# Gate and up in pairs of column slices over four k tiles, and attention's small matmuls packed into parts of the array

## The chip, the cores and the metric

The kernel runs on one core of one Trainium2 chip. The metric is the device time of one execution in microseconds (us). TensorE is PE in the profile, VectorE is DVE, ScalarE is ACT, GpSimd is POOL; PEld is the loading of weights into TensorE, which mostly runs beside the matmul before. PSUM is the memory into which this kernel's matmuls write; a place there for 512 float32 columns is called a bank here.

## The reference, cut to what matters

Four layers over x of shape 1 x 2048 x 576: attention A, MLP B, A, B, each on a layernorm of x and added to x. A is a sliding-window attention with 32 heads of 18, eight keys per query at distances 0, 2, ..., 14. B multiplies two projections, without a nonlinearity:

```python
def _B_ref(x, w_gate, w_up, w_down):          # D = 576, F = 4608
    g = jnp.einsum("bsd,df->bsf", x, w_gate)  # contraction over all 576
    u = jnp.einsum("bsd,df->bsf", x, w_up)
    h = g * u
    return jnp.einsum("bsf,fd->bsd", h, w_down)
x = x + _A_ref(_layernorm(x), A_wqkv, A_wo)
x = x + _B_ref(_layernorm(x), B_w_gate, B_w_up, B_w_down)
# ... and both once more
```

The inputs: w_gate and w_up are normal numbers times 0.05 times 576^-0.5, w_down times 0.05 times 4608^-0.5, so B adds very little to x.

## The kernel before

Tokens are worked on in chunks of 256 (CH), of two tiles of 128 (NST). 576 input features are five k tiles of 128 (KT = 5), of which the fifth holds 64 features (TL) and 64 columns that are zero in xn. F is 36 slices of 128 (NFT), called ft. The attention of one chunk is issued ahead of the MLP of another, so that their instructions are interleaved on every engine: TensorE fills with MLP matmuls while VectorE does the attention's elementwise work.

```python
# head: layernorm, transpose to xnT (features on partitions)
nc.scalar.activation(xn[:, 0:D], x[:], ACT.Identity, bias=nmr[:], scale=rstd[:])
for k in range(KT):
    nc.tensor.transpose(tps[:, k, :], xn[:, k * P:(k + 1) * P], ident[:])
nc.scalar.copy(xnT[:, :, i * P:(i + 1) * P], tps[:])
# ... attention: qkv, then per pair of window taps: products and sums on DVE, logits on PE
    nc.tensor.matmul(pa[b][:], lhsT=Erep2, rhs=s1[...], start=True, stop=True)
    for j in range(4):
        nc.scalar.copy(Lt[32 * j:32 * j + 32, ...], lgv[32 * j:32 * j + 32, :, SQ * j:SQ * (j + 1)])
# ... softmax, then the weights are broadcast over the heads' features
for j in range(4):
    b = next_pa()
    nc.tensor.matmul(pa[b][:], lhsT=Bsel[:, j]..., rhs=a_c[...], start=True, stop=True)
    nc.scalar.copy(ab[:, :, j, :], pa[b][:]...)
# ... weighted sum of v over the taps on DVE (pv, oT), then wo
# MLP
def gate_up(ft):
    ps = gu[ft % 2]                            # two PSUM banks, gate and up in one
    for (hh, w_) in ((0, wg), (1, wu)):
        for k in range(KT):
            nc.tensor.matmul(ps[:, hh, :], lhsT=w_[:, k, ft * P:(ft + 1) * P], rhs=xnT[:, k, :], ...)
    nc.scalar.copy(g_sb[:], ps[:, 0, :])
    nc.vector.tensor_tensor(hT[:], ps[:, 1, :], g_sb[:], op=ALU.mult)
def down(ft):
    for i in range(NST):                       # 512 + 64 output columns
        nc.tensor.matmul(accm[i][:], lhsT=hT[:, i * P:(i + 1) * P], rhs=wdt[:, ft % G, 0:512], ...)
        nc.tensor.matmul(acct[:, i, :], lhsT=hT[:, i * P:(i + 1) * P], rhs=wdt[:, ft % G, 512:D], ...)
gate_up(0)
for ft in range(1, NFT):
    gate_up(ft)
    down(ft - 1)
```

## Time and profile before

| | kernel before |
|---|---|
| time, median of 4 executions | 1268.28 us |
| span of the profiled execution | 1265.2 us |
| PE, DVE, ACT busy | 93%, 59%, 44% |
| gate and up matmuls | 5760 of 256 columns |
| waiting PE after the start-up | 81 of 1188 us |

The last row is not a line of any view. It comes from the trace: for each matmul the time from its start to the next matmul's start, less its step (0.109 us for 256 columns and so on, as the prediction derives it). I call the surplus a gap and name it after the matmul that follows. Streaming is the sum of the steps alone; packed matmuls that start together count as one step. Some traces lack matmul records (159 of 10032 in this one); their steps are put back. The count is finer than the profile's idle column, because the record of a matmul, 273 ns for 256 columns, covers 0.16 us beyond its step and hides short gaps.

### The profile page before, as it was taken

The page shows a single profiled execution, that of the slowest core. Times are in us where ns is not written, and L with a number is a line of the kernel's source. Part 1 is how long each engine was busy: PE and PEld are TensorE (multiplying, and loading weights), DVE is VectorE, ACT ScalarE, POOL GpSimd, SP SyncE. Part 2 cuts the span into 40 slices and gives each one's busy share as a digit, 9 for nine tenths or more (in the row PEclk, how much of TensorE's full clock was granted, in tenths as well). Part 3 has the DMA queues.
Part 4 walks back from the last instruction along what each step waited for, and adds up shares of the span by engine and source line. Part 5 has one row for each costly group of instructions (what it writes and reads, how often), then busy time and mean ns, then how long its engine had stood idle before and what let it go on. Part 6 is the DMA issues. An engine that isn't in the chain of part 4 may idle for free.

```text
span 1265.2 us, 24030 instructions
## 1 busy us (share of the span) xinstructions
PE 1176.8 (93%) x9873; PEld 874.7 (69%) x10032; DVE 745.3 (59%) x1602; ACT 559.7 (44%) x1523; POOL 4.8 (0%) x23
## 2 busy tenths in 40 slices
PE   3289999999999999999999999999999999999998
PEld 2056767767676776767677677776767777676776
DVE  4657375674737558375675736658484655837532
ACT  6263353545345354454634435354544534445321
POOL 1000000000000000000000000000000000000000
PEclk9589999999999999999999999999999999999999
DMA  7912213122231212312222231222223132221331
GB/s 265 296 28 76 81 56 92 57 76 76 76 109 57 80 57 76 95 57 76 76 76 68 75 94 57 76 67 68 83 76 81 62 88 64 76 80 57 91 103 48
DMA packets 83918, 105.95 MB, mean 84 GB/s; under 512 B 3424, under 2 KB 81888, under 8 KB 82528
## 3 DMA queue, kind: packets, MB, share of 16 engines
q1 hardware_dynamic: 83808, 104.41, 27.9%
q8 instruction: 78, 1.28, 0.4%
q14 instruction: 32, 0.26, 0.1%
HBM read 102.04 MB, written 2.36 MB: 83 GB/s over the span
## 4 chain that ended last, share of the span: by engine, by line
PE 53%; DVE 34%; ACT 10%; issue 2%; DMA 0%; SPq 0%; ACTq 0%; DVEq 0%
PE gu L299 28%; PE accm L312 10%; PE pa L201 8%; DVE oT L266 7%; DVE pv L265 7%; DVE prod L216 5%; DVE hT L305 5%; ACT ab L255 3%; PE pa L272 3%; PE acct L314 3%; PE tps L184 2%; ACT Lt L225 2%; DVE prod L217 2%; DVE st L172 1%; ACT xnb L182 1%
## 5 line engine op out<-in xcount | busy, mean ns | idle before, releaser
L305 DVE TENSOR_TENSOR hT<-gu,g_sb 128x256 bf16<-128x256 f32 x576 | 241.5, 419 | 310.8 <-ACT g_sb L304 309.9
L299 PE MATMUL gu<-xnT,wg 128*128 128x256 bf16 x2880 | 423.3, 273 | 0.0
L299 PE MATMUL gu<-xnT,wu 128*128 128x256 bf16 x2880 | 419.1, 273 | 0.0
L304 ACT CAST g_sb<-gu 128x256 bf16<-128x256 f32 x576 | 213.2, 370 | 429.2 <-PE gu L299 420.0
L312 PE MATMUL accm<-wdt,hT 128*128 128x512 bf16 x1001 | 325.0, 381 | 9.2 <-DVE hT L305 7.1
L299 PEld LDWEIGHTS <-wg 128*128 128x128 bf16 x2880 | 245.0, 98 | 90.3 <-issue 0.2
L299 PEld LDWEIGHTS <-wu 128*128 128x128 bf16 x2880 | 280.6, 98 | 36.9 <-issue 1.2
L314 PE MATMUL acct<-wdt,hT 128*128 128x64 bf16 x1152 | 221.9, 193 | 11.2 <-DVE hT L305 3.6
L312 PEld LDWEIGHTS <-hT 128*128 128x128 bf16 x1152 | 112.2, 97 | 119.2 <-DVE hT L305 40.6
L216 DVE TENSOR_TENSOR prod<-qT,kT 128x2560 bf16<-128x2560 bf16 x64 | 93.2, 1484 | 102.0 <-ACT kT L206 102.0
L201 PE MATMUL pa<-xnT,wqkv 128*128 128x256 bf16 x1200 | 144.5, 273 | 1.9 <-ACT xnT L185 1.5
L201 PEld LDWEIGHTS <-wqkv 128*128 128x128 bf16 x1200 | 117.0, 98 | 29.1 <-issue 4.5
L314 PEld LDWEIGHTS <-hT 128*128 128x128 bf16 x1152 | 112.8, 98 | 9.9 <-issue 2.0
L266 DVE TENSOR_TENSOR oT<-oT,pv 128x1280 bf16<-128x1280 bf16 x112 | 91.2, 814 | 0.7
L265 DVE TENSOR_TENSOR pv<-vT,ab 128x1280 bf16<-128x1280 bf16 x112 | 89.6, 815 | 0.0
L225 ACT COPY Lt<-pa 32x128 f32<-32x128 f32 x256 | 65.6, 256 | 34.8 <-PE pa L222 31.6
L182 ACT ACTIVATE xnb<-xf,nmr,rstd 128x576 bf16<-128x576 f32 x64 | 55.5, 869 | 11.5 <-DVE nmr L179 11.1
L272 PE MATMUL pa<-wo_p,oT 128*128 128x288 bf16 x320 | 46.1, 292 | 14.0 <-DVE oT L266 12.3
L185 ACT COPY xnT<-tps 128x640 bf16<-128x640 bf16 x64 | 44.1, 689 | 21.5 <-PE tps L184 20.4
L172 DVE BATCH_NORM_STATS2 st<-xf 128x6 f32<-128x288 f32 x128 | 51.6, 439 | 2.9 <-ACT xf L74 2.9
L184 PE MATMUL tps<-ident,xnb 128*128 128x128 bf16 x320 | 29.8, 226 | 22.2 <-ACT xnb L182 19.1
L272 PEld LDWEIGHTS <-oT 128*128 128x128 bf16 x320 | 30.5, 99 | 28.6 <-DVE oT L266 19.1
(57 smaller groups left out, 538.0 us busy)
## 6 DMA issues: line engine op xcount, KB each, us to landing
wdt<-in_B_w_down_dram SPq DMA_DIRECT2D x144, 576.0 KB, 4.0
wg<-in_B_w_gate_dram SPq DMA_DIRECT2D x4, 1152.0 KB, 9.4
wu<-in_B_w_up_dram SPq DMA_DIRECT2D x4, 1152.0 KB, 22.7
xb<-in_A_x_dram SPq DMA_DIRECT2D x16, 144.0 KB, 3.6
out_dram<-ob SPq DMA_DIRECT2D x16, 144.0 KB, 3.9
wraw<-in_A_wqkv_dram SPq DMA_DIRECT2D x4, 432.0 KB, 5.0
wg<-in_B_w_gate_dram SPq DMA_DIRECT2D x2, 576.0 KB, 17.0
wu<-in_B_w_up_dram SPq DMA_DIRECT2D x2, 576.0 KB, 23.9
```

The source lines that it names most:

```text
L182: nc.scalar.activation(xn[:, 0:D], x[:], ACT.Identity, bias=nmr[:], scale=rstd[:])
L201: nc.tensor.matmul(pa[b][:, 0:CH], lhsT=wqf[:, k, t3, t * P:(t + 1) * P], rhs=xnT[:, k, :], start=(k == 0), stop=(k == KT - 1))
L216: nc.vector.tensor_tensor(prod[:], q2, k2, op=ALU.mult)
L225: nc.scalar.copy(Lt[32 * j:32 * j + 32, 2 * p_:2 * p_ + 2, :], lgv[32 * j:32 * j + 32, :, SQ * j:SQ * (j + 1)])
L265: nc.vector.tensor_tensor(pv[:], vT[:, :, o0:o0 + CH], abw, op=ALU.mult)
L266: nc.vector.tensor_tensor(oT[:], oT[:], pv[:], op=ALU.add)
L272: nc.tensor.matmul(pa[hh][:, 0:HD], lhsT=oT[:, t, i * P:(i + 1) * P], rhs=wo_p[:, t, hh * HD:(hh + 1) * HD], start=(t == 0), stop=(t == KT ...
L299: nc.tensor.matmul(ps[:, hh, :], lhsT=w_[:, k, ft * P:(ft + 1) * P], rhs=xnT[:, k, :], start=(k == 0), stop=(k == KT - 1), skip_group_chec ...
L304: nc.scalar.copy(g_sb[:], ps[:, 0, :])
L305: nc.vector.tensor_tensor(hT[:], ps[:, 1, :], g_sb[:], op=ALU.mult)
L312: nc.tensor.matmul(accm[i][:], lhsT=hT[:, i * P:(i + 1) * P], rhs=wdt[:, ft % G, 0:512], start=(ft == 0), stop=(ft == NFT - 1))
L314: nc.tensor.matmul(acct[:, i, :], lhsT=hT[:, i * P:(i + 1) * P], rhs=wdt[:, ft % G, 512:D], start=(ft == 0 and i == 0), stop=(ft == NFT - ...
```

## The change

Its visible intent: make gate and up cheaper, with one copy and one product for two ft; use narrow matmuls in parts of the array for the logits and the broadcast of the softmax weights; lay the 64-feature tails of gate and up out in two halves of one tile. Cut to its core:

```diff
-    wu = wpool.tile([P, KT, F], BF16, name="wu")
+    wu = wpool.tile([P, KT - 1, F], BF16, name="wu")
+        nc.sync.dma_start(wg[0:TL, KT - 1, :], B_w_gate[(KT - 1) * P:D, :])
+        nc.sync.dma_start(wg[TL:P, KT - 1, :], B_w_up[(KT - 1) * P:D, :])
-    gu = [psum.tile([P, 2, CH], FP32, name=f"gu{i}") for i in range(2)]
+    gp = psum.tile([P, 2, CH], FP32, name="gp")
+    up = psum.tile([P, 2, CH], FP32, name="up")
             nc.scalar.activation(xn[:, 0:D], x[:], ACT.Identity, ...)
+            nc.gpsimd.tensor_copy(xn[:, D:DP], xn[:, D - TL:D])
 # logits: one group of four after all taps
-            nc.tensor.matmul(pa[b][:], lhsT=Erep2, rhs=s1[...], ...)
-            for j in range(4):
-                nc.scalar.copy(Lt[32 * j:32 * j + 32, ...], ...)
+        for j in range(4):
+            nc.tensor.matmul(pa[b][32 * j:32 * j + 32, :], lhsT=Esum, rhs=s1[:, :, SQ * j:SQ * (j + 1)], ...)
+        nc.scalar.copy(Lt[:], pa[b][:]...)
 # broadcast: 32 contraction rows each
-        for j in range(4): ... lhsT=Bsel[:, j] (128 rows) ...
+        for j2 in range(0, 4, 2):
+            for j in (j2, j2 + 1):
+                nc.tensor.matmul(pa[j % 2][:], lhsT=Brep[32 * j:32 * j + 32]..., rhs=a_c[32 * j:32 * j + 32]..., ...)
 # MLP
+        def gate_up(f2):
+            for ps, w_ in ((gp, wg), (up, wu)):
+                for e in range(2):
+                    for k in range(KT - 1):
+                        nc.tensor.matmul(ps[:, e, :], lhsT=w_[:, k, fs], rhs=xnT[:, k, :], ...)
+                nc.scalar.copy(g_sb[:], gp[:])
+                nc.vector.tensor_tensor(hT[:], up[:], g_sb[:], op=ALU.mult)
```

More of the change, by code (lines that the diff above doesn't have):

```diff
@@ L85 @@
     xn_bufs = [st_pool.tile([P, DP], BF16, name=f"xnb{i}") for i in range(2)]
-    for t_ in xn_bufs:
-        nc.gpsimd.memset(t_[:, D:DP], 0.0)
     wqkv = wpool.tile([P, KT, 3, DHP, 32], BF16, name="wqkv")
@@ L91, with load_rows @@
     wg = wpool.tile([P, KT, F], BF16, name="wg")
-    wu = wpool.tile([P, KT, F], BF16, name="wu")
+    wu = wpool.tile([P, KT - 1, F], BF16, name="wu")
     ksz = [min(P, D - k * P) for k in range(KT)]
     TL = D - (KT - 1) * P
-    def load_rows(dst, src):
-        for k in range(KT):
-            nc.sync.dma_start(dst[:ksz[k], k, :], src[k * P:k * P + ksz[k], :])
-        nc.sync.dma_start(dst[TL:2 * TL, KT - 1, :], src[(KT - 1) * P:D, :])
+    def load_rows(dst, src, lo=0):
+        for k in range(KT - 1):
+            nc.sync.dma_start(dst[:, k, :], src[k * P:(k + 1) * P, :])
+        nc.sync.dma_start(dst[lo:lo + TL, KT - 1, :], src[(KT - 1) * P:D, :])
     startup_pool = tc.tile_pool(name="startup", bufs=1)
@@ L112 @@
     if nlayers > 1:
-        load_rows(wg, B_w_gate)
-        load_rows(wu, B_w_up)
+        for k in range(KT - 1):
+            nc.sync.dma_start(wg[:, k, :], B_w_gate[k * P:(k + 1) * P, :])
+        nc.sync.dma_start(wg[0:TL, KT - 1, :], B_w_gate[(KT - 1) * P:D, :])
+        nc.sync.dma_start(wg[TL:P, KT - 1, :], B_w_up[(KT - 1) * P:D, :])
+        for k in range(KT - 1):
+            nc.sync.dma_start(wu[:, k, :], B_w_up[k * P:(k + 1) * P, :])
     wd_v = B_w_down.rearrange("(g t p) d -> g p t d", p=P, t=G)
@@ L133 @@
     Erep = consts.tile([P, 4, 32], BF16, name="Erep")
-    Erep2 = Erep[:].rearrange("p a b -> p (a b)")
-    Bsel = consts.tile([P, 4, 4, 32], BF16, name="Bsel")
+    Esum = Erep[:, 0, :]
+    Brep = consts.tile([P, 4, 32], BF16, name="Brep")
     n_alayers = (nlayers + 1) // 2
@@ L143, in finish_startup @@
         nc.gpsimd.memset(wqkv[:, :, :, Dh:DHP, :], 0.0)
+        nc.gpsimd.memset(wqkv[TL:P, KT - 1, :, 0:Dh, :], 0.0)
         for t_ in halo_k + halo_v:
@@ L146, in finish_startup @@
         for k in range(KT):
-            src = wraw[:, k, :].rearrange("p (t h d) -> p t d h", t=3, h=H)
+            kk = ksz[k]
+            src = wraw[:kk, k, :].rearrange("p (t h d) -> p t d h", t=3, h=H)
             if k % 2 == 0:
-                nc.vector.tensor_copy(wqkv[:, k, :, 0:Dh, :], src)
+                nc.vector.tensor_copy(wqkv[:kk, k, :, 0:Dh, :], src)
             else:
-                nc.scalar.copy(wqkv[:, k, :, 0:Dh, :], src)
+                nc.scalar.copy(wqkv[:kk, k, :, 0:Dh, :], src)
         startup_pool.__exit__(None, None, None)
@@ L156, in finish_startup @@
                                     base=-32 * g0, pattern=[[0, 4], [-1, 32]], channel_multiplier=1)
-        nc.gpsimd.memset(Bsel[:], 0.0)
-        for j in range(4):
-            nc.gpsimd.affine_select(out=Bsel[:, j], in_=Bsel[:, j], compare_op=ALU.not_equal, fill=1.0,
-                                    base=-32 * j, pattern=[[0, 4], [-1, 32]], channel_multiplier=1)
+        nc.gpsimd.tensor_copy(Brep[:], Erep[:])
         rot_box["rot"] = ctx.enter_context(tc.tile_pool(name="rot", bufs=2))
@@ L209, in phase_A @@
         nc.scalar.copy(halo_v[la][:], vT[:, :, CH:CH + HALO])
+        s1 = rot_box["rot"].tile([P, W, CH], BF16, name="s1", bufs=1)
         for p_ in range(W // 2):
@@ L217, in phase_A @@
             nc.vector.tensor_tensor(prod[:, :, 0:4:2, :], prod[:, :, 0:4:2, :], prod[:, :, 1:4:2, :], op=ALU.add)
-            s1 = rot_box["rot"].tile([P, 2, CH], BF16, name="s1", bufs=2)
-            nc.vector.tensor_tensor(s1[:], prod[:, :, 0, :], prod[:, :, 2, :], op=ALU.add)
-            nc.vector.tensor_tensor(s1[:], s1[:], prod[:, :, 4, :], op=ALU.add)
-            b = next_pa()
-            nc.tensor.matmul(pa[b][:], lhsT=Erep2, rhs=s1[:].rearrange("p w s -> p (w s)"), start=True, stop=True)
-            lgv = pa[b][:].rearrange("p (w s) -> p w s", w=2)
-            for j in range(4):
-                nc.scalar.copy(Lt[32 * j:32 * j + 32, 2 * p_:2 * p_ + 2, :], lgv[32 * j:32 * j + 32, :, SQ * j:SQ * (j + 1)])
-            yield
-            yield
+            s1v = s1[:, 2 * p_:2 * p_ + 2, :]
+            nc.vector.tensor_tensor(s1v, prod[:, :, 0, :], prod[:, :, 2, :], op=ALU.add)
+            nc.vector.tensor_tensor(s1v, s1v, prod[:, :, 4, :], op=ALU.add)
+            yield
+        b = next_pa()
+        for j in range(4):
+            nc.tensor.matmul(pa[b][32 * j:32 * j + 32, :], lhsT=Esum, rhs=s1[:, :, SQ * j:SQ * (j + 1)],
+                             start=True, stop=True)
+        nc.scalar.copy(Lt[:], pa[b][:].rearrange("p (w s) -> p w s", w=W))
+        yield
         if c == 0:
@@ L250, in phase_A @@
         yield
-        for j in range(4):
-            b = next_pa()
-            nc.tensor.matmul(pa[b][:], lhsT=Bsel[:, j].rearrange("p a b -> p (a b)"),
-                             rhs=a_c[:].rearrange("p w s -> p (w s)"), start=True, stop=True)
-            nc.scalar.copy(ab[:, :, j, :], pa[b][:].rearrange("p (w s) -> p w s", w=W))
+        for j2 in range(0, 4, 2):
+            for j in (j2, j2 + 1):
+                nc.tensor.matmul(pa[j % 2][:], lhsT=Brep[32 * j:32 * j + 32].rearrange("p a b -> p (a b)"),
+                                 rhs=a_c[32 * j:32 * j + 32].rearrange("p w s -> p (w s)"), start=True, stop=True)
+            for j in (j2, j2 + 1):
+                nc.scalar.copy(ab[:, :, j, :], pa[j % 2][:].rearrange("p (w s) -> p w s", w=W))
         yield
@@ L289, in phase_B @@
         wds = {}
-        def gate_up(ft):
-            if ft % G == 0:
-                wdt = rot_box["rot"].tile([P, G, D], BF16, name="wdt", bufs=3)
-                nc.sync.dma_start(wdt[:], wd_v[ft // G])
-                wds[ft // G] = wdt
-            ps = gu[ft % 2]
-            for (hh, w_) in ((0, wg), (1, wu)):
-                for k in range(KT):
-                    nc.tensor.matmul(ps[:, hh, :], lhsT=w_[:, k, ft * P:(ft + 1) * P], rhs=xnT[:, k, :],
-                                     start=(k == 0), stop=(k == KT - 1), skip_group_check=True)
-            g_sb = rot_box["rot"].tile([P, CH], BF16, name="g_sb", bufs=2)
-            hT = rot_box["rot"].tile([P, CH], BF16, name="hT", bufs=3)
-            with tc.high_priority():
-                nc.scalar.copy(g_sb[:], ps[:, 0, :])
-                nc.vector.tensor_tensor(hT[:], ps[:, 1, :], g_sb[:], op=ALU.mult)
-            hts[ft] = hT
@@ L308, in down @@
-        def down(ft):
-            hT = hts.pop(ft)
-            wdt = wds[ft // G]
-            for i in range(NST):
-                nc.tensor.matmul(accm[i][:], lhsT=hT[:, i * P:(i + 1) * P], rhs=wdt[:, ft % G, 0:512],
-                                 start=(ft == 0), stop=(ft == NFT - 1))
-                nc.tensor.matmul(acct[:, i, :], lhsT=hT[:, i * P:(i + 1) * P], rhs=wdt[:, ft % G, 512:D],
-                                 start=(ft == 0 and i == 0), stop=(ft == NFT - 1), skip_group_check=True)
+        def gate_up(f2):
+            for ft in (2 * f2, 2 * f2 + 1):
+                if ft % G == 0:
+                    wdt = rot_box["rot"].tile([P, G, D], BF16, name="wdt", bufs=3)
+                    nc.sync.dma_start(wdt[:], wd_v[ft // G])
+                    wds[ft // G] = wdt
+            for ps, w_ in ((gp, wg), (up, wu)):
+                for e in range(2):
+                    fs = slice((2 * f2 + e) * P, (2 * f2 + e + 1) * P)
+                    for k in range(KT - 1):
+                        nc.tensor.matmul(ps[:, e, :], lhsT=w_[:, k, fs], rhs=xnT[:, k, :],
+                                         start=(e == 0 and k == 0), stop=(k == KT - 2), skip_group_check=True)
+            g_sb = rot_box["rot"].tile([P, 2, CH], BF16, name="g_sb", bufs=2)
+            hT = rot_box["rot"].tile([P, 2, CH], BF16, name="hT", bufs=3)
+            with tc.high_priority():
+                nc.scalar.copy(g_sb[:], gp[:])
+                nc.vector.tensor_tensor(hT[:], up[:], g_sb[:], op=ALU.mult)
+            hts[f2] = hT
@@ new lines, in down @@
+        def down(f2):
+            hT = hts.pop(f2)
+            for e in range(2):
+                ft = 2 * f2 + e
+                wdt = wds[ft // G]
+                for i in range(NST):
+                    nc.tensor.matmul(accm[i][:], lhsT=hT[:, e, i * P:(i + 1) * P], rhs=wdt[:, ft % G, 0:512],
+                                     start=(ft == 0), stop=(ft == NFT - 1))
+                    nc.tensor.matmul(acct[:, i, :], lhsT=hT[:, e, i * P:(i + 1) * P], rhs=wdt[:, ft % G, 512:D],
+                                     start=(ft == 0 and i == 0), stop=(ft == NFT - 1), skip_group_check=True)
@@ L317, in phase_B @@
         gate_up(0)
         yield
-        for ft in range(1, NFT):
-            gate_up(ft)
-            down(ft - 1)
+        for f2 in range(1, NFT // 2):
+            gate_up(f2)
+            down(f2 - 1)
             yield
-        down(NFT - 1)
+        down(NFT // 2 - 1)
         for i in range(NST):
@@ L385 @@
                 n += 1
-                if n == (NFT * 2) // 3 and k + 1 < nB:
+                if n == NFT // 3 and k + 1 < nB:
                     b_head(k + 1)
```

## The prediction

> **What bounds the kernel now.** I read the page first (busy shares, slices, groups), then the timeline of TensorE in a calm stretch, then the waits, then the windows of one layer period. The busy shares and slices of the page:
>
> ```profile
> PE 1176.8 (93%) x9873; PEld 874.7 (69%) x10032; DVE 745.3 (59%) x1602; ACT 559.7 (44%) x1523; POOL 4.8 (0%) x23
> ...
> PE   3289999999999999999999999999999999999998
> ...
> PEclk9589999999999999999999999999999999999999
> ```
>
> TensorE (PE) is full from slice 3 on, at full clock; only the first 73 us (the first attention body has nothing beside it) are thin. A busy PE can still be a waiting PE, so I look at the steps between matmuls. The timeline of PE in a calm stretch:
>
> ```profile
> 212.22 0.38 PE L312 MATMUL accm<-wdt,hT 128*128 128x512 bf16 x1
> 212.44 0.19 PE L314 MATMUL acct<-wdt,hT 128*128 128x64 bf16 x1
> 212.47 0.38 PE L312 MATMUL accm<-wdt,hT 128*128 128x512 bf16 x1
> 212.68 0.19 PE L314 MATMUL acct<-wdt,hT 128*128 128x64 bf16 x1
> 212.71 0.71 PE L299 MATMUL gu<-xnT,wg 128*128 128x256 bf16 x5
> 213.26 0.71 PE L299 MATMUL gu<-xnT,wu 128*128 128x256 bf16 x5
> 213.80 0.38 PE L312 MATMUL accm<-wdt,hT 128*128 128x512 bf16 x1
> ```
>
> From start to start: five 256-wide matmuls take 0.545 us, so 0.109 us each; a 512-wide one 0.216; a 64-wide one 0.028. One ft (one 128-column slice of F) costs 10 x 0.109 + 2 x 0.244 = 1.58 us, which is 213.80 less 212.22: no gap at all. Of the PE's work, by those steps: gate and up 5760 x 0.109 = 628 us; down 1152 x 0.244 = 281; qkv 1200 x 0.109 = 131; wo 320 x 0.123 (scaled from 0.109 by 288/256) = 39; transposes 320 x 0.057 = 18; the logit matmuls (Erep) and the broadcast matmuls (Bsel), 64 each x 0.215 = 13.8 and 13.8. Sum 1125 us, about 18 of them before 73 us. The last matmul starts at 1261 us, so 1188 us of steady state hold 1107 us of streaming and 81 us of waiting PE. The waits view and the groups name part of the latter (the views give busy spans; I took the rest from start-to-start gaps):
>
> ```profile
> PEld L312 <- DVE hT L305: 40.6, 119, 0.9
> ...
> PEld L184 <- ACT xnb L182: 31.1, 37, 11.0
> ...
> PE pa L253 <- DVE a_c L249: 15.2, 16, 6.7
> ...
> PE pa L222 <- DVE s L220: 7.6, 15, 4.6
> ```
>
> Start-to-start gaps after 73 us, by what follows: hT into down about 26 us, the broadcast matmuls 16, the logit matmuls 8, transposes 9, qkv 12 (mostly 0.08 each time a pa bank is reused), wo 5, small ones 5. The second engine matters locally. Windows of one period, first the stretch from the first prod to the last oT, then the calm one:
>
> ```profile
> 162.40:198.00 35.60, 34.14 (x277) 24.08 (x280) 31.24 (x64) 16.58 (x51) 0.00 (x0) 1.00 0.24 67
> 206.00:222.00 16.00, 15.83 (x144) 12.55 (x146) 4.25 (x10) 4.39 (x13) 0.00 (x0) 1.00 0.37 111
> ```
>
> Columns: stretch, length, then busy PE, weight load, DVE, ACT, POOL. DVE (VectorE) is 88% busy in 36 of each 75 us and nearly idle in the rest: there PE and DVE run neck and neck.
>
> **What the Trainium skill says.** "TensorE: Matmul & The Clock Gate", section "Back-to-back issue gap", gives N/2.4 + 2.5 ns: 109 ns for 256 columns, 216 for 512. The trace agrees to the nanosecond; so a dropped matmul is worth its step, not its 273 ns of recorded duration. The same page, "Part 3: Packing small matmuls", lets matmuls in different 32-row or 32-column groups run at once (3 column tiles gave 2.38x); "TensorEngine Tiling (Array Packing)", "Key Properties", adds that "Changing tiling mode (not just tile) drains the TensorE". No run here shows either yet. "GPSIMD Engine Reference", "Key points": POOL shares its SBUF interfaces with VectorE. The kernel before has no POOL work in steady state.
>
> **The change, part by part.**
>
> 1. Gate and up. The kernel before contracts over five k tiles, the fifth half zero. The changed one loops over four only. Its weight tile and duplicated xn rows are laid out for a packed tail (gate in rows 0 to 63, up in rows 64 to 127), but in the instruction order no matmul reads them: there are 2304 + 2304 gate and up matmuls, all on full k tiles. So the last 64 of 576 input features are left out of gate and up. The MLP adds something tiny to x (its weights are scaled down twice), so I expect the comparison still to pass; it is less arithmetic, not the same done better. Removed: 1152 x 0.109 = 126 us, nearly all on PE in steady state.
>
> 2. Pairs. gate_up and down now handle two ft. hT: 288 of 128x512 in place of 576 of 128x256. For 512 elements out of PSUM the page's add into ob takes 686 ns, so DVE goes from 241 to 198 us. g_sb: 288 x 588 ns (the ab copy's duration) = 169 for 213 us on ACT. PSUM is no longer two alternating banks but one for gate, one for up. Gate's bank is needed again 0.87 (up) + 0.98 (down) = 1.85 us after it is filled, and the copy takes about 0.8 with drain: enough. Up's bank is needed again after 0.98 + 0.87 = 1.85 us, and DVE needs 0.2 drain + 0.69: 0.95 us of slack, about 0.55 before. But a DVE instruction run of A between two hT is now longer (in the new order three to eight of them).
>
> 3. Logits. Four matmuls with 32 output columns each, in four column groups, replace four of 128 columns; 64 remain, but the four should run at once, 16 x 0.25 = 4 us for 13.8, so -10. ACT loses 256 copies of 256 ns (66 us) and gains 16 of 0.59 (9 us), off the PE's path except at the start.
>
> 4. Broadcast. Matmuls with 32 contraction rows. In the new order the first two are adjacent, the other two stand alone between B's work, so only one pair overlaps: -3 us. Each change of tiling costs a drain, about 0.17 us (0.38 recorded less 0.216 step); some four groups per body, two switches each, partly under existing waits: I put +8 us in all.
>
> 5. The tail copy on POOL between xn and the fifth transpose. A 128x64 memset took 151 ns, so about 0.2 us plus two handovers of 0.05; four transposes cover 0.22 of it. 64 heads: +9 us, if no DVE instruction holds the port.
>
> 6. Start. One logit copy for eight of 0.26 in a row on the chain, less 0.5 for the POOL copies, fewer duplicate weight loads (about 1.4 MB, behind other work): 73 becomes about 71 us.
>
> **The waits that the new order makes.** Walking one period with measured durations: prods start 5.9 us into the 8.2 us of qkv; two prods, their adds and hT end at 12.0, before PE wants the bank at 12.3. The next pair of prods (2.9) and hT end at 15.5, PE wants it at 15.05: 0.45 lost. Then the logit matmuls wait for the last adds: 0.6. In the oT stretch three instructions of about 0.74 and one hT of about 0.6 (overlapped with their neighbours) give 2.8 us per pair against the PE's 2.72: 0.5 lost over the stretch. Together with the rest about 2 us per period, 32 us for 26. At a layer's end DVE does the x adds (1.8) and two statistics (0.8) before the first hT, which ends 3.3 us after the last down; PE wants up's bank after 2.6 us: 0.7 x 16 = +11, where two banks took it up before.
>
> Sum: streaming 1107 - 126 - 10 - 3 = 968. Waits: hT 32, boundary 11, logits 5, broadcast 16, transposes 18, qkv 12, wo 5, drains 8, small 3 = 110. Span 71 + 968 + 110 + 4 (after the last matmul) = 1153; the old median lies 3 above its span, so 1156. My allowances for drains and POOL are guesses on the high side and partly overlap; I lower it to 1150.
>
> **The rivals.**
> (a) PE stays the bound and nearly all of the removed streaming is won with no new waits: 1268 - 126 - 13 - 2 = 1127. For it: a calm stretch without gaps, more slack for hT. Against it: the neck-and-neck stretch.
> (b) DVE becomes the bound in the attention half: A's DVE work in the 36 us does not shrink. By my walk DVE needs 26.5 + 10 x 0.61 = 33 us there and PE 33 too; were DVE to have 2 us more of waiting on ACT, all periods grow: 1185.
> (c) Drains, and POOL held up by DVE's two-input instructions: 1 us per head instead of 0.15 adds 50 us, 1200. Heads fall where DVE is light, so unlikely.
> (d) Packing is not concurrent: +10, 1160.
>
> **Range and chances.** The 126 us are nearly certain, since a whole tenth of the densest stream goes; to come within 2% (above 1243) new waits would have to eat 93 us beyond what I count. 1120 is rival (a) with a bit more, 1182 is (b). Faster by over 2%: 0.97; within: 0.025; slower: 0.005.
>
> **What would show each step.** Step 1: 4608 gate and up matmuls at 0.109. Step 2: hT near 690 and g_sb near 590 ns, the calm pair at 2.72 us. Step 3 and 4: starts of four logit matmuls within some 0.05 us of each other; gaps of about 0.2 around them are drains. Step 5: the POOL copy well under 0.5 us, gaps inside groups of five transposes. Boundary: a gap of 0.7 us before the second pair's up matmuls, released by DVE hT. Wrong if gaps before up matmuls sum to well over 60 us, or if a period takes over 70 us where I count (1150 - 75)/16 = 67.

## The result, and the profile after

The changed kernel takes 1133.82 us (median of 9 executions; the fast ones 1132.81 to 1135.54), the kernel before 1267.69 (13 executions). The ratio is 0.8943, 95% interval 0.8934 to 0.8952. The prediction was 1150, range 1120 to 1182.

The execution that was profiled first took 3757.68 us. Its page shows what was slow (busy shares, then one group; mean ns of one instruction follows the busy time):

```profile
PE 3634.6 (97%) x8737; PEld 1776.4 (47%) x8880; DVE 729.4 (19%) x1314; ACT 471.1 (13%) x995; POOL 21.1 (1%) x82
...
L306 PE MATMUL up<-xnT,wu 128*128 128x256 bf16 x2304 | 1038.1, 694 | 0.0
```

Only TensorE is slow: its 256-wide step is 0.42 us in place of 0.109, while DVE and ACT durations are those of any other run, and the granted clock is recorded as 1.0. No other execution was like it. It says nothing of the change.

### e1_again: the changed kernel, profiled again

> The changed kernel once more, unedited, because its one profiled execution fell in a slow state (3756 us, matmuls of 256 columns about 0.41 us apart in place of 0.109). Expected: 1133 us, 256-wide steps of 0.109 us, hT near 690 ns, g_sb near 585 ns. By my prediction's working the waits after the start-up sum to about 110 us and there is a gap of 0.7 us at each layer's end; as the time came out 16 us lower than predicted, I expect some 95 us of waits and the missing part in the allowances for drains (8), the tail copy (9) and the layer's end (11). Rival: the extra 16 us come from streaming (the packed matmuls), not from waits.

Measured: 1135.8 us in its one execution, span 1134.0 us, granted clock 0.982. The busy shares and slices answer to those of before:

```profile
PE 1048.5 (92%) x8880; PEld 768.5 (68%) x8880; DVE 711.5 (63%) x1314; ACT 465.4 (41%) x995; POOL 21.1 (2%) x82
...
PE   3179999999999999999999999999999999999998
...
PEclk9669999999999999999999999999999999999999
```

The picture has not changed: PE is full from slice 3 on, and it is 128 us shorter in busy time. The groups whose sizes were predicted (busy us, mean ns | idle before):

```profile
L312 DVE TENSOR_TENSOR hT<-up,g_sb 128x512 bf16<-128x512 f32 x288 | 197.8, 687 | 202.5 <-PE up L306 193.3
L311 ACT CAST g_sb<-gp 128x512 bf16<-128x512 f32 x288 | 168.7, 586 | 362.8 <-PE gp L306 353.6
L306 PE MATMUL up<-xnT,wu 128*128 128x256 bf16 x2304 | 308.6, 273 | 3.3 <-DVE hT L312 0.8
```

hT was predicted at 686 ns and g_sb at 588. The windows of the attention stretch and of a calm stretch (length, then busy PE, PEld, DVE, ACT, POOL):

```profile
489.90:526.10 36.20, 34.34 (x291) 24.55 (x288) 31.24 (x49) 12.80 (x29) 0.00 (x0) 1.00 0.30 88
532.90:541.80 8.90, 8.82 (x80) 6.42 (x77) 3.38 (x10) 5.95 (x12) 0.71 (x3) 1.00 0.40 98
```

The attention stretch is as long as before, 36 us, with DVE again at 31.24 us (over bodies 2 to 16 the stretch from first prod to last oT is 36.3 us on average, 35.8 before). What has become shorter is the rest of the period, where DVE has little to do: the period is 67.4 us on average, 75.9 before. The waits that answer to those of before:

```profile
PEld L187 <- ACT xnb L184: 33.2, 38, 10.9
...
PE pa L277 <- DVE oT L271: 21.8, 16, 12.3
...
PE pa L228 <- DVE s L224: 15.6, 15, 8.4
PE pa L257 <- DVE a_c L253: 11.9, 16, 5.7
...
PEld L321 <- DVE hT L312: 2.9, 16, 0.2
```

The wait of down's weight loads for hT has gone from 40.6 to 2.9 us. In its place TensorE waits for the attention chain: for oT (wo, L277) and for the last sums (logits, L228). 12.3 and 8.4 us of these two are the start-up, where nothing else can run.

Start-to-start gaps after 73 us, in us:

| | before | changed | e2: tail alone | e7: all but the tail | e8: pairs undone | e12: three k tiles |
|---|---|---|---|---|---|---|
| streaming | 1107 | 971 | 983 | 1096 | 971 | 845 |
| gaps in all | 81 | 85 | 96 | 75 | 91 | 101 |
| of these before gate, up and down | 29 | 19 | 49 | 9 | 42 | 42 |
| before logits | 8 | 10 | 8 | 11 | 2 | 5 |
| before broadcast | 14 | 14 | 10 | 16 | 12 | 12 |
| before wo | 5 | 13 | 2 | 14 | 2 | 5 |
| before transposes | 9 | 15 | 12 | 10 | 17 | 23 |
| time, median | 1268 | 1134 | 1159 | 1252 | 1141 | 1026 |

Gaps before qkv (10 to 12 us in each of these kernels) have no row, and neither have surpluses of a few ns, so the rows do not add up to the total.

So e1_again's expectation had the right direction (some 95 us expected, 85 found), and its rival, that the surplus came from streaming, fell: 971 us of streaming against 968 predicted. The parts in which I looked for the surplus were only half right: the layer's end and the drains were smaller, but the wait before wo was larger.

### The profile page after: what moved, and what is told of

It is laid out like the page before. It is cut to its first block, busy times and chain, and to the rows that moved or that the text cites. A ratio compares the mean times of both kernels' runs of the same rounds, so it can differ in the third digit from the quotient of the medians.

```text
span 3755.9 us, 21083 instructions
## 1 busy us (share of the span) xinstructions
PE 3634.6 (97%) x8737; PEld 1776.4 (47%) x8880; DVE 729.4 (19%) x1314; ACT 471.1 (13%) x995; POOL 21.1 (1%) x82
## 4 chain that ended last, share of the span: by engine, by line
PE 96%; issue 2%; DVE 1%; ACT 0%; DMA 0%; SPq 0%; DVEq 0%
PE up L306 25%; PE gp L306 25%; PE accm L321 22%; PE pa L204 13%; PE acct L323 4%; PE pa L277 4%; PE tps L187 2%; PE pa L257 1%; PE pa L228 0%; ACT wqkv L156 0%; DVE prod L220 0%; DVE oT L271 0%; DVE pv L270 0%; DMA wraw<-in_A_wqkv_dram 0%; ACT xnb L184 0%
## 5 line engine op out<-in xcount | busy, mean ns | idle before, releaser
L306 PE MATMUL up<-xnT,wu 128*128 128x256 bf16 x2304 | 1038.1, 694 | 0.0
L306 PE MATMUL gp<-xnT,wg 128*128 128x256 bf16 x2304 | 1020.0, 682 | 0.0
L321 PE MATMUL accm<-wdt,hT 128*128 128x512 bf16 x1009 | 991.0, 1061 | 0.0
L306 PEld LDWEIGHTS <-wu 128*128 128x128 bf16 x2304 | 512.7, 224 | 426.6 <-issue 426.0
L306 PEld LDWEIGHTS <-wg 128*128 128x128 bf16 x2304 | 469.8, 212 | 493.7 <-issue 492.3
L312 DVE TENSOR_TENSOR hT<-up,g_sb 128x512 bf16<-128x512 f32 x288 | 199.1, 691 | 2153.3 <-PE up L306 2153.3
L321 PEld LDWEIGHTS <-hT 128*128 128x128 bf16 x1152 | 257.5, 224 | 553.8 <-issue 553.8
L323 PE MATMUL acct<-wdt,hT 128*128 128x64 bf16 x1152 | 445.3, 387 | 73.7 <-issue 73.7
L204 PE MATMUL pa<-xnT,wqkv 128*128 128x256 bf16 x1200 | 497.9, 693 | 0.8 <-ACT xnT L188 0.8
L311 ACT CAST g_sb<-gp 128x512 bf16<-128x512 f32 x288 | 168.5, 585 | 2048.5 <-PE gp L306 2047.9
L323 PEld LDWEIGHTS <-hT 128*128 128x128 bf16 x1152 | 207.3, 180 | 67.5 <-issue 67.5
L277 PE MATMUL pa<-wo_p,oT 128*128 128x288 bf16 x320 | 157.2, 742 | 12.5 <-DVE oT L271 12.4
L277 PEld LDWEIGHTS <-oT 128*128 128x128 bf16 x320 | 70.3, 220 | 88.6 <-issue 75.0
## 6 DMA issues: line engine op xcount, KB each, us to landing
wg<-in_B_w_gate_dram SPq DMA_DIRECT2D x1, 576.0 KB, 14.8
```

The lines of the kernel that those rows point to most:

```text
L204: nc.tensor.matmul(pa[b][:, 0:CH], lhsT=wqf[:, k, t3, t * P:(t + 1) * P], rhs=xnT[:, k, :], start=(k == 0), stop=(k == KT - 1))
L277: nc.tensor.matmul(pa[hh][:, 0:HD], lhsT=oT[:, t, i * P:(i + 1) * P], rhs=wo_p[:, t, hh * HD:(hh + 1) * HD], start=(t == 0), stop=(t == KT ...
L306: nc.tensor.matmul(ps[:, e, :], lhsT=w_[:, k, fs], rhs=xnT[:, k, :], start=(e == 0 and k == 0), stop=(k == KT - 2), skip_group_check=True)
L311: nc.scalar.copy(g_sb[:], gp[:])
L312: nc.vector.tensor_tensor(hT[:], up[:], g_sb[:], op=ALU.mult)
L321: nc.tensor.matmul(accm[i][:], lhsT=hT[:, e, i * P:(i + 1) * P], rhs=wdt[:, ft % G, 0:512], start=(ft == 0), stop=(ft == NFT - 1))
```

## The experiments

Every kernel here gave the reference's result within the comparison's tolerance unless it says otherwise. That is weaker than it sounds, as the last one shows.

### e2_tail: only the dropped k tile

```diff
-                for k in range(KT):
+                for k in range(KT - 1):          # in the kernel before; stop moved to match
```

> The kernel before with one edit: gate and up run over four k tiles in place of five, so the same arithmetic is left out as in the changed kernel (the result is then as wrong as its result). Theory (the dropped matmuls are nearly the whole gain): 1268 - 126 = 1142 us, between 1138 and 1150. Rival (pairs and one-bank buffers are needed to collect it, since the old 576 hT instructions keep VectorE even with TensorE in the attention half): half of the period is bound by VectorE and keeps its time, so only about 60 to 90 us are won: 1178 to 1208.

Measured: 1158.72 us, ratio 0.914, interval 0.9125 to 0.9155: 110 us won, neither 126 nor 60 to 90. The streaming shrank by 124 us as it should (1107 to 983), and gaps rose by 15. Their place shows in the waits for hT (total us, times, longest):

```profile
PEld L312 <- DVE hT L305: 68.1, 167, 1.1
PE accm L312 <- DVE hT L305: 21.2, 49, 0.8
```

Before, the first of these was 40.6 us in 119 waits. My reading: in the attention stretch VectorE has a fixed amount to do, and a shorter gate_up asks for hT sooner than VectorE can come back to it. About seven eighths of a dropped matmul step is collected, the rest turns into this wait.

### e7_fulltail: all of the change but the dropped k tile

```diff
-    wu = wpool.tile([P, KT - 1, F], BF16, name="wu")
+    wu = wpool.tile([P, KT, F], BF16, name="wu")   # tail loaded twice, as before; xn's spare columns zero
-                    for k in range(KT - 1):
+                    for k in range(KT):
-            nc.gpsimd.tensor_copy(xn[:, D:DP], xn[:, D - TL:D])
```

> The changed kernel with the tail as a full fifth k tile, zero-padded as before (complete arithmetic), the zeros in xn set once, no copy on GpSimd, one input buffer fewer to make room. This is the change without its dropped matmuls. Theory: 1134 + 126 - about 5 for the missing copy = 1255, so the rest of the change (pairs, packed logits, packed broadcast) is worth some 10 to 15 us, about 1% against the kernel before. Rival: the rest is worth nothing, or pairs cost: 1265 to 1280. Other rival: pairs are worth much in combination: under 1235.

Measured: 1252.09 us, ratio 0.987, interval 0.9856 to 0.9885, as the theory said (1255). The changed kernel leaves out 64 of 576 features of gate and up; with complete arithmetic the rest of the change is worth 1.3%. From this kernel to the changed one it is 118 us for 126 us of dropped steps: more is collected than without pairs. This kernel also lacks the copy on GpSimd and has one input buffer fewer; against e4_nopool below, which lacks the copy too, it is 120 us (0.0945 of 1268).

### e3_packed and e9_twice: the tail in two halves of the array

The layout of the changed kernel (gate's tail in rows 0 to 63 of a tile, up's in rows 64 to 127) invites this:

```diff
+            for e in range(2):                       # between gate's and up's full tiles
+                nc.tensor.matmul(gp[:, e, :], lhsT=wg[0:TL, KT - 1, fss[e]], rhs=xnT[0:TL, KT - 1, :], ...)
+                nc.tensor.matmul(up[:, e, :], lhsT=wg[TL:P, KT - 1, fss[e]], rhs=xnT[TL:P, KT - 1, :], ...)
```

> The changed kernel plus the tail that it leaves out, packed: per pair four matmuls of 64 contraction rows, gate in rows 0 to 63 and up in rows 64 to 127, adjacent, into different banks; the arithmetic of the reference is complete again. If the two halves run at once and a change of tiling costs nothing: 288 x 2 x 0.109 = +63 us, 1197. If they run at once but each entry and exit drains about 0.17 us: +63 + 98 = 1295, which would be slower than the kernel before. If they do not overlap and nothing drains: +126, 1259. I lean to overlap with small drains: 1200 to 1230.

Measured: 1254.57 us, ratio 0.9891, interval 0.9877 to 0.9906. That is the time of e7, whose tail costs four full matmuls per pair. The timeline of PE in the packed kernel shows why:

```profile
561.06 0.60 PE L305 MATMUL gp<-xnT,wg 128*128 128x256 bf16 x4
561.59 0.28 PE L308 MATMUL gp<-xnT,wg 64*128 64x256 bf16 x1
561.60 0.28 PE L310 MATMUL up<-xnT,wg 64*128 64x256 bf16 x1
561.71 0.27 PE L308 MATMUL gp<-xnT,wg 64*128 64x256 bf16 x1
561.72 0.27 PE L310 MATMUL up<-xnT,wg 64*128 64x256 bf16 x1
561.92 0.28 PE L314 MATMUL up<-xnT,wu 128*128 128x256 bf16 x1
```

The two halves do run at once: they start 4 ns apart in the trace. But the full matmul ahead of the group has a step of 0.205 us, and the step out of the group is 0.202, each some 0.095 above 0.109. Those two surpluses and the group's two steps (0.12 and 0.109) come to about 0.42 us per pair beyond the full matmul's own step; four full matmuls cost 0.436. Half the steps are saved, and two changes of tiling take it all back. My lean (1200 to 1230) was wrong, since I expected drains to be small; the estimate with drains of 0.17 was too dark.

The weight loads show where the surplus lies. The timeline of PEld in the same place:

```profile
561.28 0.10 PEld L305 LDWEIGHTS <-wg 128*128 128x128 bf16 x1
561.59 0.09 PEld L308 LDWEIGHTS <-wg 64*128 64x128 bf16 x1 [0.21 <-issue]
...
561.91 0.11 PEld L314 LDWEIGHTS <-wu 128*128 128x128 bf16 x2 [0.21 <-issue]
```

The load at 561.28 runs beside the full matmul before the one that it serves, which starts at 561.39. At each change of tiling the load starts only 4 ns before its own matmul, after 0.21 us without a load. A load's record is 0.09 to 0.10 us long, as long as the surplus. So what is paid can be a drain or a load that is no longer hidden; no run separates the two. Below, "drain" stands for either.

To see whether it is the change of tiling, e9 makes two visits per pair in place of one, with the same matmuls:

```diff
                 for k in range(KT - 1):
                     nc.tensor.matmul(gp[:, e, :], lhsT=wg[:, k, fss[e]], ...)
-            for e in range(2):
                 nc.tensor.matmul(gp[:, e, :], lhsT=wg[0:TL, KT - 1, fss[e]], ...)
```

> The packed tail once more (complete arithmetic), with two visits to 64-row tiling per pair in place of one: the tail of the first ft follows its gate matmuls, that of the second follows its own. Same matmuls, same operands. In the trace of the packed tail both halves start 4 ns apart, and the first step into and the first step out of the group are each 0.096 us longer. Theory (a fixed drain at each change of tiling): 288 more visits x 2 x 0.096 = +55: 1254.6 + 55 = 1310, between 1300 and 1318. Rival (the extra step belongs to the first matmul of a bank, or to a smaller weight load, not to the change of tiling): within 10 us of 1255.

Measured: 1281.38 us, ratio 1.0107, interval 1.0092 to 1.0122: slower than the kernel before, +27 us, between the theory and its rival. The steps say that the surplus is paid at every visit, as the theory had it, and where the other half went. The timeline of PE:

```profile
560.46 0.60 PE L305 MATMUL gp<-xnT,wg 128*128 128x256 bf16 x4
560.99 0.28 PE L307 MATMUL gp<-xnT,wg 64*128 64x256 bf16 x1
561.00 0.28 PE L309 MATMUL up<-xnT,wg 64*128 64x256 bf16 x1
561.21 0.61 PE L305 MATMUL gp<-xnT,wg 128*128 128x256 bf16 x4
```

The surplus recurs at each visit: some 575 steps into a group at a median of 0.205 us, and as many out of one at 0.212. The second visit starts no new bank, and inside e3's groups a 64-row load follows a 64-row load with a step of 0.12, so neither the bank nor the smaller load by itself makes it. Gaps before gate and up sum to 118 us in place of 61, so +57, near the +55 expected. But gaps before wo, logits, broadcast and transposes fell from 52 to 26 us: TensorE now arrives later where it used to wait for VectorE's chain. In this kernel a loss on TensorE is partly paid from those waits, just as a gain is partly lost to them.

### e4_nopool: without the copy on GpSimd

```diff
+    for t_ in xn_bufs:
+        nc.gpsimd.memset(t_[:, D:DP], 0.0)
-            nc.gpsimd.tensor_copy(xn[:, D:DP], xn[:, D - TL:D])
```

> The changed kernel without the tail copy on GpSimd: the 64 spare columns of xn are zeroed once at the start, as before. Nothing reads the copied values with weight (the rows of wqkv below are zero, gate and up do not read the fifth tile), so the output does not change. Theory: the copy delays the fifth transpose of each head; the start-to-start gaps before and inside transposes were 14.8 us in the changed kernel, 8.7 in the one before: -6, and -1 at the start: 1127, between 1124 and 1130. Rival: other work of TensorE hides it, within 2 us of 1134. Prediction on record: +9 for the copy.

Measured: 1131.11 us, ratio to the kernel before 0.8925, interval 0.8911 to 0.8938. Against the changed kernel's 0.8943 that is a difference of 0.0018 of 1268, 2.3 us, and the intervals touch. Gaps before transposes fell from 14.8 to 12.1 us, not by 6. So the copy costs some 2 us at most, nearer to the rival. A copy took 236 ns in the trace, and four transposes beside it take 4 x 0.056 us. In the profiled executions about 1 us of it is the start: the first gate matmul starts at 70.2 us in place of 71.2.

### e5_logits and e6_bcast: the packed parts undone, one at a time

```diff
 # e5: the logit matmuls of before, per pair of taps, and eight small copies on ACT per two of them
+            nc.tensor.matmul(pa[b][:], lhsT=Erep2, rhs=s1[:]..., start=True, stop=True)
 # e6: the broadcast of before
+            nc.tensor.matmul(pa[b][:], lhsT=Bsel[:, j]..., rhs=a_c[:]..., start=True, stop=True)
```

> The changed kernel with the logit part of before: four full-width logit matmuls in four steps, eight small copies on ScalarE per two of them. Theory (streaming and waits of TensorE): four packed matmuls take 0.33 us from the first start to the next other matmul, four plain ones 0.86, so +0.53 x 16 = +8.5, and the waits in front stay near 9 us: 1142 to 1146. Rival A: the 56 us of ScalarE come back into the chain and add 1 us or more per period: 1155. Rival B: ending the last copies earlier helps the softmax chain: no change.

> The changed kernel with the broadcast part of before: four full 128-row matmuls. In the trace of the changed kernel a lone 32-row matmul takes 0.30 to 0.32 us from its start to the next, a plain one 0.215, and an adjacent pair 0.32. So packed costs 0.32 + 2 x 0.31 = 0.94 per body, plain 0.86: undoing it gains 16 x 0.08 = 1 us. Theory: 1131 to 1134, same within noise. Rival: the saved streaming of 3 us as predicted: 1137 or more.

Measured: e5 1146.16 us, ratio 0.9037 (0.9022 to 0.9052), so +0.0094 of 1268 = 12 us for undoing the packed logits. In the profiled executions the span is 10.7 us longer: the streaming rose by 10 us, and the gaps stayed (85.6 for 85.2). e6 1131.21 us, ratio 0.8924 (0.8911 to 0.8937): undoing the packed broadcast gains about 2 us, where 0 to 3 were expected (the interval overlaps that of the changed kernel, 0.8934 to 0.8952, so the gain is hardly more than noise). Both are 32-wide parts of the array, and the difference is company. The timeline of PE in the changed kernel, first the logits:

```profile
502.60 0.40 PE L228 MATMUL pa<-s,Erep 128*32 128x512 bf16 x4 [0.47 <-DVE s L224]
502.93 0.39 PE L306 MATMUL gp<-xnT,wg 128*128 128x256 bf16 x2
```

Four matmuls of 512 columns take 0.33 us from their start to the next matmul, for 4 x 0.215 = 0.86 plain. Then two lone broadcasts:

```profile
509.99 0.37 PE L257 MATMUL pa<-a_c,Brep 32*128 32x512 bf16 x1
510.29 0.39 PE L306 MATMUL up<-xnT,wu 128*128 128x256 bf16 x2
510.61 0.38 PE L257 MATMUL pa<-a_c,Brep 32*128 32x512 bf16 x1
```

A lone one takes 0.31 us to the next matmul for 0.215 plain, because it is alone in its tiling and pays for the way out by itself. It pays for the way in too, which my expectation left out: the two matmuls before the second one take 0.32 us for 0.218.

### e8_nopairs: pairs undone

```diff
-        def gate_up(f2): ...                     # gp, up: one bank each, hT of 512 columns
+        def gate_up(ft): ...                     # gu[ft % 2], hT of 256 columns, still four k tiles
```

> The changed kernel with pairs undone: one ft at a time, gate and up together in one bank, two banks alternating, 576 hT of 256 columns; four k tiles as in the changed kernel, packed logits, packed broadcast and the copy on GpSimd kept. Theory: pairs pay where VectorE and TensorE run neck and neck; waits before down were 49 us in the kernel before with the tail dropped and waits before up and down 16 us in the changed one, so +30: 1155 to 1167. Rival: the packed logits, which free ScalarE, are what removed those waits: 1134 to 1142.

Measured: 1141.42 us, ratio 0.9002, interval 0.8989 to 0.9015: pairs are worth 0.0059 of 1268 = 7.5 us, not the 21 to 33 of the theory; the rival's number was right. Its reason was not: with the packed logits kept, gaps before gate, up and down are 42 us against 19 with pairs, so it is pairs that remove 23 us of waits for hT, as my theory said. But the gaps before wo and logits are 11 and 8 us smaller without pairs. With the hT waits in its way TensorE seems to arrive at wo later, when oT is ready. My theory counted the waits that go and not those that come in their place.

### e11_tap: less work for VectorE

```diff
-        for i_ in range(W):
+        for i_ in range(W - 1):                  # last tap left out of the weighted sum
```

> The changed kernel with the last of the eight window taps left out of the output sum: a wrong result on purpose, two VectorE instructions of 0.74 us (overlapped) fewer per attention body, TensorE's work unchanged. Theory (TensorE is the bound, VectorE costs only the waits before wo, up and the broadcast, some 12.7 + 8 us that depend on it): -4 to -14: 1120 to 1130. Rival A (VectorE is the bound in the attention stretch, each us off it is a us off the period): -24: 1110. Rival B (TensorE's order is made anew, and its waits with it): no change, 1132 to 1136.

Measured: 1131.42 us, ratio 0.8926 (0.8911 to 0.8941), 2 us less, with intervals that overlap. Its output is wrong, which doesn't matter for the time. The gain is smaller than the theory expected, and the time is near rival B's. Some 24 us of VectorE's time (2 x 0.74 x 16) went and the gaps on TensorE hardly changed in sum (83 for 85): before wo they stayed at 13 to 14. The two traces show why. Without the tap the attention stretch is 34.5 us on average in place of 36.3, but the period is 67.4 us in both: what VectorE gives back, the rest of the period takes. The profiled span is 4.8 us shorter, of which 4.6 lie before the second attention body, whose first prod starts at 78.5 us in place of 83.1 (and e1_again's execution was 2 us above the median). wo is issued after the shorter stretch, so its wait stayed. So VectorE's work sets the length of the attention stretch and not that of the period; rival A is out.

### e12_three: one more k tile left out

```diff
-                    for k in range(KT - 1):
+                    for k in range(KT - 2):
```

> The changed kernel with one more k tile left out of gate and up (three of five): wrong on purpose, another 1152 x 0.109 = 126 us of matmul steps less, nothing else edited. It asks how much of a dropped step is still collected, and whether the comparison notices. So far 126 us dropped gave 110 without pairs (waits before down rose by 20) and 118 with pairs. Theory (TensorE stays the bound, waits at VectorE rise further): 100 to 115 us less, 1019 to 1034. Rival (VectorE becomes the bound in the attention stretch, half the period): 60 to 80 less, 1054 to 1074. I expect the comparison to pass still, since the MLP adds so little to x.

Measured: 1025.89 us, ratio 0.8092, interval 0.8079 to 0.8106: 108 us less for 126 of dropped steps, as the theory said. The streaming falls by 126 to 845, the gaps rise by 16. And the comparison passes with 192 of 576 features missing from gate and up. So its passing the changed kernel does not show that leaving out 64 is harmless; it shows that a loss of a third of gate's and up's features is not seen with these inputs. An estimate from the reference's scales says why: on a normalized x, g and u are about 0.05 in size, h 0.0025, and B's output 0.000125, beside an x that begins at 0.05.

### e10_best: what the single edits left

The changed kernel without the copy on GpSimd, with the plain broadcast, and without the fifth weight tile that nothing reads.

> The changed kernel with what the single edits showed to be of no use taken out: no tail copy on GpSimd, the plain broadcast, no fifth weight tile loaded or stored (nothing reads it); pairs and packed logits stay. Theory: the two gains add, 2.7 + 2.6: 1134 - 5 = 1129, 1127 to 1130, ratio to the kernel before 0.889 to 0.891. Rival: both shorten the same wait, 1131.

Measured: 1129.27 us, ratio 0.8904, interval 0.8891 to 0.8917, against 0.8943 for the changed kernel: 5 us less, clear of the changed kernel's interval, as if the two gains add; what the unread weight tile costs was not measured by itself. It beats both kernels in time, with the same arithmetic missing as in the changed one. Of those that compute everything, e7_fulltail is the fastest that was run, at 1252 us.

## Why the prediction was right

The mechanism and the class were right, and the time came out 16 us below the predicted one. Step by step:

1. Gate and up. As predicted: 2304 + 2304 matmuls at a step of 0.109. The dropped 126 us are the gain nearly whole; alone they brought 110 (e2), on top of the rest 118 (e7 to the changed kernel).
2. Pairs. The durations were right within 2 ns. Their worth in the final kernel is 7.5 us (e8).
3. Logits. The prediction had -10 from four at once at 0.25 us; they took 0.33, which is -8.5, and undoing the part costs 12 us.
4. Broadcast. -3 for streaming and +8 for drains gave +5, where the 8 include those around the logits; undoing the broadcast gains about 2. The sign was right. The drain was put at 0.17 us, the part of a matmul's record beyond its step, and measured about 0.1.
5. The copy on GpSimd. +9 predicted, about +2 measured: the mean copy of 236 ns was near the estimate, but gaps before transposes were at most a few us larger for it. The prediction's sum was off too: 0.2 + 0.1 - 0.22 us for each of 64 heads is 5, not 9.
6. Start. 71 predicted; the first gate matmul started at 71.2 us against 69.7 before, so the start got longer, not shorter, and the steady state still begins at 73. A small miss, and a sign error.
7. The waits of the new order. This is the term that was mis-sized: 110 us predicted, 85 measured, while streaming was 971 for 968. The two parts "hT 32" and "boundary 11", 43 together, came out as 19. (In the kernel before, the recount has 29 us before gate, up and down and 14 before the broadcast, where the prediction had 26 and 16.) wo, put at 5, came out as 13, and the logits' wait at 10 for 5.

73 + 971 + 85 and 4 us after the last matmul give 1133, the measured span. The prediction's own terms gave 1153 for the span, 1156 for the time, before it was lowered to 1150 by judgement. The difference is the waits (-25), streaming (+3) and the start (+2). That lowering went the right way, but no run stood behind it. The signs of being wrong stayed away: the mean period is 67.4 us for 67 counted.

Why the boundary came out small can be read in the timeline of DVE at a layer's end in e1_again:

```profile
475.29 0.69 DVE L341 TENSOR_TENSOR xf<-accm,xf 128x512 f32<-128x512 f32 x1 [0.97 <-PE accm L321]
...
476.62 0.21 DVE L342 TENSOR_TENSOR xf<-acct,xf 128x64 f32<-128x64 f32 x1
476.75 0.81 DVE L174 BATCH_NORM_STATS2 st<-xf 128x6 f32<-128x288 f32 x2
477.48 0.67 DVE L312 TENSOR_TENSOR hT<-up,g_sb 128x512 bf16<-128x512 f32 x1
```

The order is the predicted one: x adds, two statistics, hT. But the chain takes 2.86 us (475.29 to 478.15). I had added recorded durations to 3.3, and consecutive DVE instructions overlap by some 0.1 us: the statistics start at 476.75, before the add that began at 476.62 with a duration of 0.21 is over. TensorE wanted the bank at 477.98, 2.6 us after the last down as predicted, and got it about 0.2 later, at 478.20. Such a gap of 0.14 to 0.23 us stands at nine of the sixteen layer ends, about 2 us in all for 11: at six others a head's transposes and qkv come before the second up, and after the last nothing follows.

Rival (a), the full gain without new waits, was 1127 and is the nearer one in number: the gaps were 85 for 81. But it was not that no wait changed: hT gave 10 back, wo and logits took 9, transposes 6. Rival (b), VectorE as the bound, is refuted by e11 and e12. Rival (c), 1 us per head through GpSimd, by e4; the contention with VectorE that "GPSIMD Engine Reference", "Key points", names was hardly put to the test, since the 64 copies of 236 to 238 ns ran beside hT (21 times), the layernorm's small instructions or nothing, and never beside attention's products and sums. Rival (d), no concurrency, by the logits' starts, 3 to 4 ns apart in the trace.

## What to carry to other kernels

Price a removed matmul at its start-to-start step and expect to collect most of it, not all, if another engine runs neck and neck for a part of the period: here 108 to 120 us of 126. Packing narrow matmuls pays by the group: four at once saved 0.53 us with the way out paid, and the way in costs about 0.1 more; four half-height ones saved nothing, and one alone lost. Check what a faster kernel no longer computes before praising it, and do not take a passing comparison as proof where the part in question is small beside a residual.

## What the Trainium skill lacked or had wrong

- "TensorEngine Tiling (Array Packing)", "Key Properties", says that a change of tiling drains the TensorE and gives no size. Here the surplus is about 0.096 us on the way into a 64-row or 32-row group and 0.09 to 0.11 on the way out of 64-row, 32-row and 32-column ones; e9 shows that it is paid per visit. Whether a drain or a weight load that is no longer hidden makes it stays open.
- "TensorE: Matmul & The Clock Gate", "Part 3: Packing small matmuls": starts some 4 ns apart are confirmed (3 to 4 ns). It gives no cost for the way in and out, and between full-height matmuls a group of two half-height pairs came out at about 0.42 us for 0.436 plain.
- The same page, "Back-to-back issue gap", gives two figures for 512 columns: about 131 ns sustained in a real kernel, and about 216 for an isolated one. In this kernel, with a weight load for every matmul, 216 ns is the step throughout, and 56 ns for 128 columns (the transposes) where the page's sustained figure is about 81.
- The same page, "Seeing it yourself", warns that clock records are unreliable and that the clock has been seen stuck at a quarter for over 50 us. One execution here (3756 us) had steps of 0.42 us for 0.109 in the median over its whole length, with the clock recorded as 1.0. That is consistent with such a state, held far longer than the page says; no run shows its cause.
